# Local products and products with the state trade visits in a gated recurrence beside an MLP

## The chip, the cores and the metric

The kernel runs on 1 core of one Trainium2 chip. The metric is the device time of one execution in microseconds (us). The kernel before takes 926.75 us, the median of 3 runs (925.89 to 927.98).

## The reference

A gated recurrence over 768 steps, for 4 batches and 8 heads of 48, whose output (as 3072 tokens of 384) goes through two MLPs with 2048 hidden columns, the first with softplus, the second with mish. Cut to what matters:

```python
f = 1.0 / (1.0 + np.exp(-f_logit))
for t in range(S):
    state = f[:, :, t, :, None] * state + np.einsum('bhd,bhe->bhde', k[:, :, t], v[:, :, t])
    y[:, :, t] = np.einsum('bhd,bhde->bhe', q[:, :, t], state)
x = y.transpose(0, 2, 1, 3).reshape(B * S, H * D)
h = x @ w_in                                            # first MLP
x = (np.maximum(h, 0.0) + np.log1p(np.exp(-np.abs(h)))) @ w_out
h = x @ w_in                                            # second MLP, its own weights
sp = np.where(h > 20.0, h, np.log1p(np.exp(np.minimum(h, 20.0))))
y = (h * np.tanh(sp)) @ w_out
```

## The kernel before

**The recurrence.** The 768 steps are cut into 6 chunks of 128 (NC); a chunk of one batch is a group g, so there are 24 groups of 8 heads in 4 head pairs, groups 4k to 4k+3 making the chunk k (the first chunk is 0 in the code; the text counts from 1, so groups 8 to 23 are "chunk 3 on"). A group is halved into two times 64 steps. For it the kernel needs the scores of q against k within each half (`a_near`, L469), the state's part of each half, k against v (L480), a running sum of the decayed state and these parts (`mid`, L491, after the first half; `state`, L506, after the second), the masked scores (L497), the local products of masked scores with v (L524) and the products of q with the decayed state `sp` and with `mid` (L532). Local products and products with the state add up in the same PSUM bank.

The matmuls of a group are small, 64 by 64 or less, and run on a quarter of PE's array each, four at a time (`TILES`). Local products take the row half h of the array for the bank h, products with the state the other row half for some. So `a_far` puts a drain of PE (L541) between the two kinds.

**The preparation of a group** is its gate: exponentials of f (ScalarE, `a_exp`), a scan on VectorE (L303) with a reciprocal (L309, `a_scan`), the inverse (ScalarE, `a_inv`), q and k scaled (VectorE, `a_q` L333, `a_k` L339), the state's decay to `sp` (`a_decay`, L354), and the turn: four transposes of k on PE (L403) and a copy by ScalarE to `kn` (L409).

**The MLPs.** The output of four groups is one tile of 512 columns. Each layer goes through 6 such tiles, 16 blocks f of hidden columns each: 96 units a layer, 192 in all. A unit is `m_h` (9 matmuls of 128x512, L636, or plain float32 ones for the first 12 units), its activation on ScalarE and VectorE (L665 to L686 in layer 1), a split into high and low parts (L651, L656), and `m_o` (9 matmuls, L766) of the unit three before, into three accumulators. After 16 units the accumulators are moved out by ScalarE (L786) and VectorE (L787). The tile's input is split into xh (ScalarE) and xl (VectorE, L610, one piece each of three) before `m_h` of the tile's first unit. Chunk k's groups run beside the units of tile k-1, since tile k needs them.

**What sets the order.** A table of hooks: `at(i, place, fn, ...)` puts a step at a place of unit i. Places in a unit come in the order `pe1` (after `m_h`), `act0`, then `m_o`, then `pe2`, then the steps of the activation, then `dve1`, `act`, `dve2`, `pe3`, `end`. From unit 14 (HAND1) the order written is the order on PE, VectorE and ScalarE; before that a scheduler moves instructions. A group of chunk 3 on is planned by `plan_hand(g, i)`, with i from `BASES`: 16, 20, 23, 26 for the first four, then 30, 34, 38, 42 and so on every 16 units. The first visit on PE (`a_near`) stands at `pe2` of unit i, its steps on VectorE (`a_nears`: mid, two masks, state) at `dve2` of unit i, the second visit (`a_far`) at `pe2` of unit i+1. The preparation of g+1 stands at units i to i+3 beside it. `plan_attn` does the same for groups 4 to 7.

Beside these run the loads and the conversion of layer 2's weights to a high and a low part (VectorE, L172, L178, L184). A second path, for gates out of range, is chosen at the end and isn't run here.

Of the kernel before, what the change touches and what calls it, by code (L numbers as in the profile page):

```python
# [8 lines left out]
F32 = mybir.dt.float32  # L9
# [16 lines left out]
R = 112  # L26
HC = C // 2
# [39 lines left out]
def recurrence__then__softplus_mish_mlps_kernel(  # L67
# [10 lines left out]
    nc = tc.nc  # L78
# [8 lines left out]
    const = pool("const")  # L87
# [3 lines left out]
    at_p = pool("at", 2)  # L91
# [6 lines left out]
    ps_o = pool("ps_o", 3, PSUM)  # L98
    ps_a = pool("ps_a", 1, PSUM)

    ident = const.tile([128, 128], F32, name="ident")
    mask = const.tile([128, C], F32, name="mask")
    near = const.tile([128, HC], F32, name="near")
    cap = const.tile([128, NP, C + 1], F32, name="cap")
# [152 lines left out]
    G = {}  # L257
# [84 lines left out]
    def a_decay(g):  # L342
        t = G[g]
        if g < B:
            return
        sp = at_p.tile([R, NP, D], F32, tag="sp", name="sp")
        if g < 2 * B:
            for p in range(NP):
                act.activation(
                    out=sp[:, p], in_=states[g % B][:, p], func=AF.Copy, scale=t["p"][:, p:p + 1]  # L350
                )
            t["sp"] = sp
# [5 lines left out]
        t["sp"] = sp  # L358
# [79 lines left out]
    def a_out(g, pl=None):  # L438
        t = G[g]
        t["yps"] = ps = bank(pl or ps_a, [128, NP, C])  # L440
        for p in range(KD, NP):
            for i in range(2):
# [3 lines left out]
                    start=(p == KD), stop=True,  # L446
                )

    def two_banks(g):
        by_hand = g >= 2 * B  # L450
        return [bank(ps_a, [128, 4 * C], f"a{z}" if by_hand else None) for z in range(2)]
# [8 lines left out]
    TILES = ((0, 0), (1, 1), (0, 1), (1, 0))  # L460

    def a_near(g):

        t = G[g]
        t["xps"] = banks = two_banks(g)
        for p in range(NP):
            for i, h in TILES:
                o, e = 64 * i, 64 * h
                pe.matmul(  # L469
                    banks[i][e:e + HC, p * HC:(p + 1) * HC],  # L470
                    t["k"][o:o + D, p, h * HC:(h + 1) * HC], t["q"][o:o + D, p, h * HC:(h + 1) * HC],
                    start=True, stop=True,
                )
        last = g >= (NC - 1) * B
        for p in range(NP):
            for h, i in TILES:
                if last and h:
                    continue
                o, e, m = 64 * i, 64 * h, D if i else 64
                pe.matmul(  # L480
                    banks[h][o:o + m, NP * HC + p * D:NP * HC + (p + 1) * D],
                    t["kn"][e:e + HC, p, o:o + m],
                    t["v"][e:e + HC, (2 * p + i) * D:(2 * p + i + 1) * D],
                    start=True, stop=True,
                )

    def a_first(g):
        t = G[g]
        t["mid"] = mid = at1.tile([R, NP, D], F32, tag="kn", name="mid")
        part = t["xps"][0][:R, NP * HC:NP * (HC + D)].rearrange("r (p d) -> r p d", p=NP)  # L490
        dve.tensor_tensor(out=mid, in0=t["sp"], in1=part, op=ALU.add)  # L491

    def a_near_mask(g, i):
        t = G[g]
        if i == 0:
            t["a"] = at_p.tile([128, 2, NP, HC], F32, tag="a", name="a")
        dve.tensor_tensor(  # L497
            out=t["a"][:, i], in0=t["xps"][i][:, 0:NP * HC].rearrange("s (p t) -> s p t", p=NP),
            in1=near.rearrange("s (o t) -> s o t", o=1).to_broadcast([128, NP, HC]), op=ALU.mult,
        )  # L500

    def a_second(g):
        t = G[g]
        if g < (NC - 1) * B:
            part = t["xps"][1][:R, NP * HC:NP * (HC + D)].rearrange("r (p d) -> r p d", p=NP)
            dve.tensor_tensor(out=states[g % B], in0=t["mid"], in1=part, op=ALU.add)  # L506
# [7 lines left out]
    def a_far(g):  # L514

        t = G[g]
        t["yps"] = banks = two_banks(g)

        def to(h, o, p, n):
            return banks[h][64 * o:64 * o + n, p * HC:(p + 1) * HC]  # L520

        def local(h, o, p):
            i, e = h ^ o, 64 * h
            return pe.matmul(  # L524
                to(h, o, p, 64), t["v"][e:e + HC, (2 * p + i) * D:(2 * p + i) * D + 64],
                t["a"][e:e + HC, i, p], start=(p == 0), stop=False,
            )

        def far(h, o, p):
            i = h ^ o  # L530
            e = 64 * i
            return pe.matmul(  # L532
                to(h, o, p, D), t["mid" if h else "sp"][e:e + D, p],
                t["q"][e:e + D, p, h * HC:(h + 1) * HC], start=False, stop=(p == NP - 1),
            )

        for p in range(NP):
            for o in (1, 0):
                for h in range(2):
                    done = local(h, o, p)  # L540
        gap = pe.drain()  # L541
        order_only(gap, done)
        for p in range(NP):
            for o in (1, 0):
                for h in range(2):
                    order_only(far(h, o, p), gap)

    def a_rest(g):
        t = G[g]
# [39 lines left out]
                nc.sync.dma_start(out=x[64 * i + 48:64 * i + 64, kk], in_=x[o:o + 16, KD])  # L589

    states = [const.tile([R, NP, D], F32, name=f"state{b}") for b in range(B)]


    xh, xl = {}, {}
# [228 lines left out]

    def plan_attn(g, i):

        at(i, "pe1", a_turn, g)
        at(i, "pe1", a_turned, g)
        at(i, "pe2", a_near, g)
        at(i, "pe2", a_nears, g)
        at(i + 1, "pe2", a_far, g)  # L830
        at(i + 2, "act0", a_outed, g)
        if g + 2 < NC * B:
            at(i + 2, "dve2", a_load, g + 2)

    def plan_hand(g, i):

        close = g < 3 * B
        at(i - 1, "pe3" if close else "pe1", a_turn, g)
        if g == 2 * B:
            at(i - 1, "end", a_turned, g)  # L840
        else:
            at(i if close else i - 1, "act0" if close else "act", a_turned, g)
        at(i, "pe2", a_near, g)
        at(i, "dve2", a_nears, g)
        at(i + 1, "pe2", a_far, g)
# [4 lines left out]
        if g == NC * B:  # L850
            at(i + 3, "dve1", judge)
            return
# [7 lines left out]
        at(i + 3, "dve1", a_decay, g)  # L860

    def plan_split(k):
        if k == 1:
# [4 lines left out]
        for kk in range(KD):  # L868
            at(k * NF - 3 + (kk > 0), "act", split_xa, (1, k), kk)
            at(k * NF - 2 + (kk > 0), "dve2" if kk == 0 else "dve1", split_xb, (1, k), kk)  # L870

    for k in range(2, n1):
        for j in range(B):
            plan_hand(k * B + j, k * NF + BASES[k > 2][j])
        i = k * NF
        at(i - 4, "act", a_fill, k)
        plan_split(k)
# [81 lines left out]
    for o in (0, 64):  # L959
        nc.gpsimd.tensor_copy(out=near[o:o + HC], in_=mask[o:o + HC, o:o + HC])  # L960
    sel = st_p.tile([128, KD, 128], F32, tag="raw", name="sel")
    nc.gpsimd.memset(sel, 0.0)

# [34 lines left out]
    with tc.manual_schedule(engines=HAND | {mybir.EngineType.SP}):  # L998
        for step in HEAD.split():
            one(step)  # L1000
    run(-1, "act0")
    run(-1, "act")

# [289 lines left out]
```

## Time and profile before

| | |
|---|---|
| median of 3 runs | 926.75 us (925.89 to 927.98) |
| the profiled execution | 925.63 us |
| its span | 923.9 us |
| PE busy | 903.1 us (98%) |
| VectorE (DVE) busy | 779.2 us (84%) |
| ScalarE (ACT) busy | 757.2 us (82%) |
| GpSimd (POOL) busy | 23.7 us (3%) |
| drains of PE (L541) | 20 |

The profile is of one execution; its span is the time from the first to the last instruction, 1.7 us less than the execution's own time. PE's clock was granted in full all through. An engine's idle time before an instruction is put down to whatever released it last. Matmuls overlap and their ends are modelled, so a standstill of PE is read from the starts of two matmuls.

### The profile page before, as it was taken

What the parts mean: (1) busy time and instruction counts of PE and PEld (TensorE: products, weight loads), DVE (VectorE), ACT (ScalarE), POOL (GpSimd) and SP (SyncE); (2) the same over time, 40 slices, a digit from 0 to 9 for tenths busy, and PEclk for the clock granted to TensorE, in tenths of its full rate; (3) what the DMA queues carried; (4) which work ended last, traced back from release to release, by engine and by line L of the source; (5) the groups of instructions that cost most, each with busy time, mean ns of one, the idle gap of its engine ahead of it and who ended that gap; (6) DMA issues with size and microseconds to landing.
All of it is one profiled execution on the core that took longest, in us unless ns stands there. A gap on an engine that the chain in (4) does not pass through costs nothing.

```text
span 923.9 us, 16281 instructions
## 1 busy us (share of the span) xinstructions
PE 903.1 (98%) x6238; PEld 704.5 (76%) x6238; DVE 779.2 (84%) x1263; ACT 757.2 (82%) x1365; POOL 23.7 (3%) x68
## 2 busy tenths in 40 slices
PE   9899998999999999999999999999999999999997
PEld 8444576777887777788888888888888888888885
DVE  8999998888889889897987898887877878877875
ACT  5887799888888888897878888877878887887875
POOL 0000000000000000000012200000000000000000
PEclk9999999999999999999999999999999999999999
DMA  9999523125345345533497660201101002000001
GB/s 309 348 358 324 181 97 109 49 78 189 132 150 182 108 143 169 181 123 112 169 325 257 226 219 5 98 1 52 52 1 69 35 1 70 34 1 1 35 1 38
DMA packets 32822, 116.19 MB, mean 126 GB/s; under 512 B 4096, under 2 KB 7168, under 8 KB 32736
## 3 DMA queue, kind: packets, MB, share of 16 engines
q1 hardware_dynamic: 27552, 96.19, 30.7%
q0 software_dynamic: 5184, 18.88, 6.3%
q8 instruction: 51, 0.84, 0.4%
q14 instruction: 35, 0.29, 0.1%
HBM read 90.48 MB, written 23.59 MB: 123 GB/s over the span
## 4 chain that ended last, share of the span: by engine, by line
PE 80%; DVE 10%; ACT 6%; issue 2%; DMA 1%; SPq 0%; DVEq 0%; ACTq 0%
PE po L766 38%; PE ps L636 36%; DVE d L673 1%; DVE d L679 1%; PE ps L469 1%; PE busy L981 1%; ACT e L666 1%; PE ps L532 1%; ACT d L667 1%; PE ps L524 1%; ACT e L665 1%; PE ps L403 1%; PE ps L480 1%; DVE w L226 1%; DMA win<-in_w_dram 1%
## 5 line engine op out<-in xcount | busy, mean ns | idle before, releaser
L636 PE MATMUL ps<-x,w 128*128 128x512 f32 x864 | 214.0, 392 | 0.0
L766 PE MATMUL po<-ghi,w 128*128 128x512 f32 x744 | 195.7, 394 | 3.2 <-DVE o L787 3.1
L636 PEld LDWEIGHTS ps<-x,w 128*128 128x128 f32 x864 | 162.3, 188 | 36.9
L636 PE MATMUL ps<-xh,w 128*128 128x512 f32 x504 | 175.2, 402 | 0.0
L766 PEld LDWEIGHTS po<-ghi,w 128*128 128x128 f32 x744 | 138.5, 188 | 34.5 <-DVE o L787 4.9
L766 PE MATMUL po<-g,w 128*128 128x512 f32 x504 | 126.1, 394 | 0.0
L700 ACT ACTIVATE l<-d 128x512 f32<-128x512 f32 x96 | 60.7, 632 | 68.6 <-DVE d L696 68.6
L636 PEld LDWEIGHTS ps<-xh,w 128*128 128x128 f32 x504 | 94.6, 188 | 22.3 <-issue 0.7
L766 PEld LDWEIGHTS po<-g,w 128*128 128x128 f32 x504 | 94.9, 188 | 21.5
L766 PE MATMUL po<-glo,w 128*128 128x512 f32 x372 | 109.0, 392 | 0.0
L636 PE MATMUL ps<-xl,w 128*128 128x512 f32 x252 | 99.0, 393 | 0.4 <-DVE xl L610 0.4
L696 DVE TENSOR_SCALAR d<-ps 128x512 f32<-128x512 f32 x96 | 66.2, 690 | 32.1 <-PE ps L636 32.1
L710 DVE SCALAR_TENSOR_TENSOR l<-d,l 128x512 f32<-128x512 f32 x96 | 66.5, 693 | 31.3 <-ACT l L703 31.0
L665 ACT ACTIVATE e<-ps 128x512 f32<-128x512 f32 x96 | 56.8, 592 | 43.2 <-DVE d L673 25.5
L656 DVE TENSOR_TENSOR glo<-l,ghi 128x512 fp32r<-128x512 f32 x124 | 85.1, 686 | 6.2 <-ACT ghi L651 5.9
L766 PEld LDWEIGHTS po<-glo,w 128*128 128x128 f32 x372 | 69.9, 188 | 15.4
L651 ACT CAST ghi<-l 128x512 fp32r<-128x512 f32 x124 | 75.0, 605 | 4.4 <-DVE l L686 4.0
L673 DVE SCALAR_TENSOR_TENSOR d<-d,e 128x512 f32<-128x512 f32 x96 | 65.7, 685 | 9.5 <-ACT d L667 8.6
L733 DVE TENSOR_TENSOR l<-ps,l 128x512 f32<-128x512 f32 x96 | 66.3, 691 | 8.5 <-ACT l L730 0.4
L679 DVE TENSOR_TENSOR d<-l,d 128x512 f32<-128x512 f32 x96 | 65.8, 686 | 0.1
L725 DVE SCALAR_TENSOR_TENSOR l<-d,l 128x512 f32<-128x512 f32 x96 | 65.4, 682 | 0.0
L666 ACT ACTIVATE e<-e 128x512 f32<-128x512 f32 x96 | 60.7, 632 | 2.8
(124 smaller groups left out, 1305.1 us busy)
## 6 DMA issues: line engine op xcount, KB each, us to landing
raw<-in_w_dram SPq DMA_DIRECT2D x32, 768.0 KB, 7.3
win<-in_w_dram SPq DMA_DIRECT2D x17, 767.9 KB, 7.2
raw<-in_w_dram SPq DMA_DIRECT2D x15, 767.9 KB, 12.0
qk<-in_qkT_dram SPq DMA_DIRECT2D x22, 448.0 KB, 4.9
x2d<-o SPq DMA_DIRECT2D x12, 768.0 KB, 3.5
w2d<-wo SPq DMA_DIRECT2D x24, 384.0 KB, 2.6
x<-x2d POOLq DMA_DIRECT2D x12, 768.0 KB, 5.5
w<-w2d POOLq DMA_DIRECT2D x24, 384.0 KB, 4.1
```

What stands on the lines that cost most here:

```text
L636: pe.matmul(ps, w, r, start=(i == 0), stop=(i == len(steps) - 1))
L651: act.copy(out=t["hi"], in_=t["g"])
L656: dve.tensor_tensor(out=t["lo"], in0=t["g"], in1=t["hi"].bitcast(F32), op=ALU.subtract)
L665: act.activation(out=e, in_=t["h"], func=AF.Abs)
L666: act.activation(out=e, in_=e, func=AF.Exp, scale=-1.0)
L673: dve.scalar_tensor_tensor(out=d, in0=d, scalar=1.0, in1=t["e"], op0=ALU.subtract, op1=ALU.subtract)
L679: dve.tensor_tensor(out=d, in0=l, in1=d, op=ALU.subtract)
L696: dve.tensor_scalar(out=t["t"], in0=t["h"], scalar1=20.0, scalar2=None, op0=ALU.min)
L710: dve.scalar_tensor_tensor(out=t["l"], in0=t["t"], scalar=-43.0, in1=t["l"], op0=ALU.max, op1=ALU.add)
L725: dve.scalar_tensor_tensor(out=t["l"], in0=t["t"], scalar=-1.0, in1=t["l"], op0=ALU.mult, op1=ALU.max)
L733: dve.tensor_tensor(out=t["l"], in0=t["h"], in1=t["l"], op=ALU.mult)
L766: pe.matmul(acc[c], w[layer, f][:, cols[c]], t[part], start=(f == 0 and part == "hi" and w is whi), stop=(f == NF - 1 and part == "lo"),)
```

## The change

For groups 8 to 23 the two visits of PE are dealt out anew.

- The visit at unit i (`a_one`) has the scores and the products with the state. Both are ready there, since `sp` and `mid` are made earlier.
- The visit at unit i+1 (`a_two`) has the local products and the state parts of the next group, g+1. VectorE's sums (`a_part_sums`: mid and state) follow it, at `dve2` of unit i+1, and are group g+1's.
- So products with the state open the sums in a bank in one visit, and local products close them in the next; there is no drain. The 20 drains become 4, those of groups 4 to 7 (`a_close`).
- The parts of group 8 stand alone in a visit at unit 16 (`a_begin`), and the first i is 17 instead of 16. The last group's second visit has no next parts.
- The products with the state have 64 columns of their stationary instead of 48, so `sp` and `mid` have 16 columns behind them; they become parts of fixed tiles (`sps`, `middle`) that they share with the constants `cap`, `mask` and `ident`, whose names the trace and the order rows then show.
- Everything that prepares a group runs one group further ahead (`plan_ahead(g + 2, i)`), its turn too; that of group 9 stands at unit 13 and is moved by the scheduler.
- q and k of g+2 are loaded at the end of unit i, v at the end of unit i+1 (both at `dve2` of unit i+2 before).
- Groups 5 to 7 have their turn and their first visit half a unit to a unit earlier.

```diff
-BASES = ((-16, -12, -9, -6), (-18, -14, -10, -6))
+BASES = ((-15, -12, -9, -6), (-18, -14, -10, -6))
...
-    def a_nears(g):
-        a_first(g)
-        a_near_mask(g, 0)
-        a_near_mask(g, 1)
-        a_second(g)
...
+    def a_begin(g):
+
+        a_parts(g, two_banks(g))
+
+    def a_one(g):
+
+        G[g]["yps"] = banks = two_banks(g)
+        a_near(g, banks, W)
+        for p in range(NP):
+            for h, o in ORDER:
+                far(g, h, o, p, True)
+
+    def a_two(g):
+
+        for p in range(NP):
+            for h, o in ORDER:
+                local(g, h, o, p)
+        if g + 1 < NC * B:
+            a_parts(g + 1, G[g]["yps"])
...
-    def plan_hand(g, i):
-
-        close = g < 3 * B
-        at(i - 1, "pe3" if close else "pe1", a_turn, g)
...
-        at(i, "pe2", a_near, g)
-        at(i, "dve2", a_nears, g)
-        at(i + 1, "pe2", a_far, g)
-        at(i + 2, "act0", a_outed, g)
-        if g + 2 < NC * B:
-            at(i + 2, "dve2", a_load, g + 2)
-        g += 1
...
+    def plan_ahead(g, i):
+
         at(i - (i % NF == 2), "act", a_exp, g)
         at(i + 1, "dve1", a_scan, g)
         at(i + 1, "act", a_inv, g)
...
+    def plan_hand(g, i, after):
+
+        if g == 2 * B:
+            at(i - 2, "pe1", a_turn, g)
+            at(i - 2, "act", a_turned, g)
+            at(i - 1, "pe2", a_begin, g)
+            at(i - 1, "dve2", a_part_sums, g)
...
+        at(i, "pe2", a_one, g)
+        at(i, "dve2", a_near_masks, g)
...
+        at(i + 1, "pe2", a_two, g)
+        if g + 1 < NC * B:
+            at(i + 1, "dve2", a_part_sums, g + 1)
...
+        if g + 2 < NC * B:
+            plan_ahead(g + 2, i)
+            close = after == i + 3
+            at(after - 1, "pe3" if close else "pe1", a_turn, g + 2)
```

PE before, the second visit of a group of chunk 4 (`a` are masked scores, `vt` is v; the drain between the two kinds isn't listed):

```order
L766 MATMUL po<-ghi,w 128x512 x6
L766 MATMUL po<-glo,w 128x512 x3
L524 MATMUL ps<-a,vt 64x64 x16
L532 MATMUL ps<-qk,sp 48x64
L532 MATMUL ps<-qk,mid 48x64
L532 MATMUL ps<-qk,sp 48x64
```

PE with the change, the end of the first visit of such a group and the second visit (`cap` and `ident` stand for the state and mid behind them):

```order
L531 MATMUL ps<-qk,cap 64x64
L672 MATMUL ps<-xh,w 128x512
L672 MATMUL ps<-xl,w 128x512
L672 MATMUL ps<-xh,w 128x512 x2
L672 MATMUL ps<-xl,w 128x512
L672 MATMUL ps<-xh,w 128x512 x2
L672 MATMUL ps<-xl,w 128x512
L672 MATMUL ps<-xh,w 128x512
L802 MATMUL po<-ghi,w 128x512 x6
L802 MATMUL po<-glo,w 128x512 x3
L521 MATMUL ps<-a,vt 64x64 x16
L477 MATMUL ps<-vt,kn 64x48
```

The products with the state have gone a unit ahead of the local products, with 18 big matmuls between, and the state parts follow the local products.

VectorE before, at the end of a tile (units 46 to 48, a chunk boundary; `gg` is the scan's result). One xl stands just ahead of these rows:

```order
L491 TENSOR_TENSOR mid<-sp,ps 112x192
L497 TENSOR_TENSOR a<-ps,near 128x256 x2
L506 TENSOR_TENSOR state_109<-mid,ps 112x192
L172 TENSOR_TENSOR wo<-raw 128x768
L178 TENSOR_SCALAR raw<-wo 128x768
L184 SCALAR_TENSOR_TENSOR wo<-win,raw 128x768
L673 SCALAR_TENSOR_TENSOR d<-d,e 128x512
L656 TENSOR_TENSOR glo<-l,ghi 128x512
L679 TENSOR_TENSOR d<-l,d 128x512
L686 SCALAR_TENSOR_TENSOR l<-ps,d 128x512
L610 TENSOR_TENSOR xl<-x,xh 128x512 x2
L303 SCALAR_TENSOR_TENSOR gg<-f,cap 112x516
```

VectorE with the change, the same place. The two masks (L509) stand just ahead of these rows, and the state's sum (L490) just behind:

```order
L646 TENSOR_TENSOR xl<-x,xh 128x512
L177 TENSOR_TENSOR wo<-raw 128x768
L183 TENSOR_SCALAR raw<-wo 128x768
L189 SCALAR_TENSOR_TENSOR wo<-win,raw 128x768
L709 SCALAR_TENSOR_TENSOR d<-d,e 128x512
L692 TENSOR_TENSOR glo<-l,ghi 128x512
L715 TENSOR_TENSOR d<-l,d 128x512
L722 SCALAR_TENSOR_TENSOR l<-ps,d 128x512
L308 SCALAR_TENSOR_TENSOR gg<-f,cap 112x516
L314 RECIPROCAL tots<-gg 112x4
L646 TENSOR_TENSOR xl<-x,xh 128x512 x2
L488 TENSOR_TENSOR ident<-mask,ps 112x192
```

The masks stand ahead of the first xl, the scan and its reciprocal ahead of the other two, and the two sums behind them.

VectorE before, ahead of the first tile's accumulators (unit 19):

```order
L333 TENSOR_TENSOR qk<-qk,gg 112x512
L339 TENSOR_TENSOR qk<-qk,f 112x512
L240 TENSOR_TENSOR w<-w_624,w 128x768
L673 SCALAR_TENSOR_TENSOR d<-d,e 128x512
L787 TENSOR_TENSOR o<-po,o 128x512 x3
```

VectorE with the change, the same place:

```order
L308 SCALAR_TENSOR_TENSOR gg<-f,cap 112x516
L314 RECIPROCAL tots<-gg 112x4
L245 TENSOR_TENSOR w<-w_619,w 128x768
L488 TENSOR_TENSOR ident<-mask,ps 112x192
L490 TENSOR_TENSOR state_109<-ident,ps 112x192
L709 SCALAR_TENSOR_TENSOR d<-d,e 128x512
L823 TENSOR_TENSOR o<-po,o 128x512 x3
```

A scan, of group 10, and the sums of group 9 stand ahead of the accumulators' move; the scan of group 9 and its q and k stand further up.

## Rows read from the trace of the kernel before

**Rows 1.** The page: busy engines (share of span), and the chain that ended last

```profile
PE 903.1 (98%) x6238; PEld 704.5 (76%) x6238; DVE 779.2 (84%) x1263; ACT 757.2 (82%) x1365; POOL 23.7 (3%) x68
...
PE 80%; DVE 10%; ACT 6%; issue 2%; DMA 1%; SPq 0%; DVEq 0%; ACTq 0%
```

**Rows 2.** Timeline of PE, both visits of one group (start us, length us, engine, line, tiles)

```profile
242.62 0.69 PE L469 MATMUL ps<-qk 48*64 48x64 f32 x32
243.14 0.63 PE L480 MATMUL ps<-vt,kn 64*64 64x48 f32 x32
243.70 0.51 PE L636 MATMUL ps<-xh,w 128*128 128x512 f32 x1
...
248.04 0.69 PE L524 MATMUL ps<-a,vt 64*64 64x64 f32 x32
248.88 0.25 PE L532 MATMUL ps<-qk,sp 48*48 48x64 f32 x1
...
249.47 0.51 PE L636 MATMUL ps<-xh,w 128*128 128x512 f32 x1
```

**Rows 3.** The drain's line: duration min/median/max in ns, first and last start

```profile
L541 PEldq DRAIN  x20: 516/587/615, 47.9 to 429.5; - x20
```

**Rows 4.** Timelines of PE and VectorE, unit 19 [idle before <- released by]

```profile
142.66 0.74 PE L766 MATMUL po<-ghi,w 128*128 128x512 f32 x2 [2.20 <-DVE o L787]
...
141.92 1.89 DVE L787 TENSOR_TENSOR o<-po,o 128x512 fp32r<-128x512 f32 x3 [0.82 <-ACT o L786]
```

**Rows 5.** Timeline of PE, standstills around three chunk boundaries

```profile
289.73 0.63 PE L636 MATMUL ps<-xh,w 128*128 128x512 f32 x2
290.55 0.50 PE L636 MATMUL ps<-xl,w 128*128 128x512 f32 x1 [0.19 <-DVE xl L610]
...
295.70 0.39 PE L636 MATMUL ps<-xh,w 128*128 128x512 f32 x1
296.42 0.57 PE L403 MATMUL ps<-ident,qk 112*128 112x112 f32 x4 [0.34 <-DMA win<-in_w_dram]
296.77 1.40 PE L766 MATMUL po<-ghi,w 128*128 128x512 f32 x5
...
225.09 0.39 PE L636 MATMUL ps<-xh,w 128*128 128x512 f32 x1
225.91 0.74 PE L766 MATMUL po<-ghi,w 128*128 128x512 f32 x2 [0.43 <-DVE o L787]
...
370.69 0.63 PE L636 MATMUL ps<-xh,w 128*128 128x512 f32 x2
371.23 0.51 PE L636 MATMUL ps<-xl,w 128*128 128x512 f32 x1
...
386.83 0.39 PE L636 MATMUL ps<-xh,w 128*128 128x512 f32 x1
387.35 0.74 PE L766 MATMUL po<-ghi,w 128*128 128x512 f32 x2
```

**Rows 6.** Timeline of VectorE, a scan and what follows its reciprocal

```profile
132.51 1.22 DVE L303 TENSOR_TENSOR_SCAN gg<-f,cap 112x516 f32<-112x516 f32 x1
...
133.87 0.93 DVE L240 TENSOR_TENSOR w<-w,w 128x768 fp32r<-128x768 f32 x1
```

**Rows 7.** Timeline of VectorE, a chunk boundary from the first visit's end

```profile
283.62 0.35 DVE L491 TENSOR_TENSOR mid<-sp,ps 112x192 f32<-112x192 f32 x1 [0.68 <-PE ps L480]
283.89 0.75 DVE L497 TENSOR_TENSOR a<-ps,near 128x256 f32<-128x256 f32 x2
284.56 0.34 DVE L506 TENSOR_TENSOR state<-mid,ps 112x192 f32<-112x192 f32 x1
284.82 0.95 DVE L172 TENSOR_TENSOR wo<-raw 128x768 fp32r<-128x768 f32 x1
...
289.81 1.28 DVE L610 TENSOR_TENSOR xl<-x,xh 128x512 fp32r<-128x512 f32 x2
291.01 1.23 DVE L303 TENSOR_TENSOR_SCAN gg<-f,cap 112x516 f32<-112x516 f32 x1
```

More of the change, by code (lines that the diff above doesn't have):

```diff
@@ L99, in recurrence__then__softplus_mish_mlps_kernel, with behind @@
     ps_a = pool("ps_a", 1, PSUM)
[L101 to L104, printed above, removed]
+    def behind(n, name):
+        both = const.tile([128, NP * D + n], F32, name=name)
+        return both[:R, 0:NP * D + 16], both[:, NP * D:]
+    middle, ident = behind(128, "ident")
+    sp1, mask = behind(C, "mask")
+    sp0, cap = behind(NP * (C + 1), "cap")
+    cap = cap.rearrange("s (p t) -> s p t", p=NP)
+    sps = [sp0, sp1]
     tots = const.tile([128, NC * B, NP], F32, name="tots")
@@ L357, in a_decay @@
         )
-        t["sp"] = sp
     n_a = [0]
@@ L447, in a_out, with chained @@
                 )
+    TILES = ((0, 0), (1, 1), (0, 1), (1, 0))
+    W = NP * HC
+    def chained(g):
+        return g >= 2 * B
     def two_banks(g):
-        by_hand = g >= 2 * B
-        return [bank(ps_a, [128, 4 * C], f"a{z}" if by_hand else None) for z in range(2)]
+        return [bank(ps_a, [128, 4 * C], f"a{z}" if chained(g) else None) for z in range(2)]
     def order_only(x, y):
@@ L458, in order_only, with a_parts @@
         )
-    TILES = ((0, 0), (1, 1), (0, 1), (1, 0))
-    def a_near(g):
+    def a_parts(g, banks):
         t = G[g]
[L465 to L474, printed above, removed]
+        t["sps"] = banks
         for p in range(NP):
             for h, i in TILES:
-                if last and h:
+                if g >= (NC - 1) * B and h:
                     continue
@@ L480, in a_near, with a_part_sums @@
                 pe.matmul(
-                    banks[h][o:o + m, NP * HC + p * D:NP * HC + (p + 1) * D],
-                    t["kn"][e:e + HC, p, o:o + m],
-                    t["v"][e:e + HC, (2 * p + i) * D:(2 * p + i + 1) * D],
+                    banks[h][o:o + m, W + p * D:W + (p + 1) * D], t["kn"][e:e + HC, p, o:o + m],
+                    t["v"][e:e + HC, (2 * p + i) * D:(2 * p + i + 1) * D], start=True, stop=True,
+                )
+    def a_part_sums(g):
+        t = G[g]
+        parts = [
+            x[:R, W:W + NP * D].rearrange("r (p d) -> r p d", p=NP) for x in t["sps"]
+        ]
+        mid = heads_of(middle)
+        dve.tensor_tensor(out=mid, in0=heads_of(t["sp"]), in1=parts[0], op=ALU.add)
+        if g < (NC - 1) * B:
+            dve.tensor_tensor(out=states[g % B], in0=mid, in1=parts[1], op=ALU.add)
@@ L484, in a_near @@
+    def a_near(g, banks, at_col):
+        t = G[g]
+        t["aps"] = [x[:, at_col:at_col + W].rearrange("s (p t) -> s p t", p=NP) for x in banks]
+        for p in range(NP):
+            for i, h in TILES:
+                o, e, half = 64 * i, 64 * h, slice(h * HC, (h + 1) * HC)
+                z = i ^ h if chained(g) else i
+                pe.matmul(
+                    t["aps"][z][e:e + HC, p], t["k"][o:o + D, p, half], t["q"][o:o + D, p, half],
                     start=True, stop=True,
@@ L485, in a_near, with a_near_masks @@
                 )
-    def a_first(g):
+    def a_near_masks(g):
         t = G[g]
[L489 to L493, printed above, removed]
-        t = G[g]
[L495 to L499, printed above, removed]
+        t["a"] = at_p.tile([128, 2, NP, HC], F32, tag="a", name="a")
+        for z in range(2):
+            dve.tensor_tensor(
+                out=t["a"][:, z], in0=t["aps"][z],
+                in1=mask[:, 0:HC].rearrange("s (o t) -> s o t", o=1).to_broadcast([128, NP, HC]),
+                op=ALU.mult,
+            )
@@ L500, in a_near_mask, with to, local, far @@
+    def to(g, h, o, p, n):
+        return G[g]["yps"][h][64 * o:64 * o + n, p * HC:(p + 1) * HC]
+    def local(g, h, o, p, first=False):
+        t = G[g]
+        i, e = h ^ o, 64 * h
+        return pe.matmul(
+            to(g, h, o, p, 64), t["v"][e:e + HC, (2 * p + i) * D:(2 * p + i) * D + 64],
+            t["a"][e:e + HC, o if chained(g) else i, p],
+            start=first and p == 0, stop=not first and p == NP - 1,
         )
-    def a_second(g):
+    def far(g, h, o, p, first=False):
@@ L503, in a_second @@
         t = G[g]
-        if g < (NC - 1) * B:
-            part = t["xps"][1][:R, NP * HC:NP * (HC + D)].rearrange("r (p d) -> r p d", p=NP)
-            dve.tensor_tensor(out=states[g % B], in0=t["mid"], in1=part, op=ALU.add)
-    def a_nears(g):
-        a_first(g)
-        a_near_mask(g, 0)
-        a_near_mask(g, 1)
-        a_second(g)
[L514 to L535, printed above, removed]
+        i = h ^ o
@@ new lines, in far, with a_open, a_opened, a_close @@
+        e = 64 * i
+        return pe.matmul(
+            to(g, h, o, p, 64), (middle if h else G[g]["sp"])[e:e + D, p * D:p * D + 64],
+            t["q"][e:e + D, p, h * HC:(h + 1) * HC],
+            start=first and p == 0, stop=not first and p == NP - 1,
+        )
+    ORDER = ((0, 0), (1, 0), (1, 1), (0, 1))
+    def a_open(g):
+        banks = two_banks(g)
+        a_near(g, banks, 0)
+        a_parts(g, banks)
+    def a_opened(g):
+        a_part_sums(g)
+        a_near_masks(g)
+    def a_close(g):
+        G[g]["yps"] = two_banks(g)
@@ L537, in a_far @@
         for p in range(NP):
-            for o in (1, 0):
-                for h in range(2):
-                    done = local(h, o, p)
+            for h, o in ORDER:
+                done = local(g, h, o, p, True)
         gap = pe.drain()
@@ L543, in a_far @@
         for p in range(NP):
-            for o in (1, 0):
-                for h in range(2):
-                    order_only(far(h, o, p), gap)
+            for h, o in ORDER:
+                order_only(far(g, h, o, p), gap)
+    def a_begin(g):
[4 more added lines that the diff above has]
+        for p in range(NP):
+            for h, o in ORDER:
+                far(g, h, o, p, True)
+    def a_two(g):
+        for p in range(NP):
+            for h, o in ORDER:
+                local(g, h, o, p)
+        if g + 1 < NC * B:
+            a_parts(g + 1, G[g]["yps"])
     def a_rest(g):
@@ L1000, in recurrence__then__softplus_mish_mlps_kernel @@
             one(step)
+    nc.gpsimd.tensor_copy(out=mask[HC:C, 0:HC], in_=mask[HC:C, HC:C])
     run(-1, "act0")
```

41 lines of the change are left out of this document (23 added, 18 removed).

## The prediction

> **What bounds the kernel now.** I read the page's busy times and chain first, then the chain's own engine in order of time, then the instructions that it waits for. TensorE (PE) is busy 98% of the span and carries 80% of the chain that ended last; VectorE (DVE) is busy 84% and carries 10% [rows 1]. So whatever shortens PE's stream should show in the time, unless PE then arrives early at something that DVE delivers. Both parts matter here, and they have to be priced apart.
>
> In the timeline of one group the reader is to see three things [rows 2]. The first visit goes from 242.62 to the next 512-column matmul at 243.70: 0.52 us of scores, 0.56 of state parts, 1.08 together, with no gap where the one kind of tile follows the other. The second goes from 248.04 to 249.47, 1.43 us. Each of the two holds 32 records of small matmuls, then 32 more; the difference is 0.35. In the second, the first product with the state starts 0.84 after the first local product, where the scores need 0.52 before the parts start; that 0.32 is the drain. The drain's own row says 0.59 [rows 3], but a part of it runs while the local products are still going through, so 0.59 is not the price.
>
> PE's standstills are the second thing, read as start to start between 512-column matmuls, which follow each other every 0.23 us. The column of idle time in the rows understates them, since matmul ends are modelled.
>
> **The change, part by part.**
>
> *The drain.* In groups 8 to 23 it goes. A group then has scores (0.52) and products with the state (248.88 to 249.47, 0.59) in the one visit, local products (0.52, taken as the scores, since they have as many records and as many columns) and parts (0.56) in the other: 2.19 against 1.08 + 1.43 = 2.51 [rows 2]. That is **0.32 us a group**. The products with the state now have a stationary of 64 columns instead of 48, which by the scores' pace (0.52 for 32 records of that width) costs nothing. The ends are nothing, if the array has to empty anyway, and 0.59, the drain's row; 0.32 is what the row nearest to the operation gives.
>
> *Where it counts.* The saving of group 8 lies ahead of the standstill at 142.66, where PE waits 2.20 us for VectorE to move the finished accumulators (L787) out [rows 4]. So does the added visit for the parts of group 8 alone, 0.56 us and its entry: the standstill covers both (without that cover the visit would cost its 0.56). Behind it 15 groups are left: 15 x 0.32 = **-4.8**. The last group's second visit has no next parts: **-0.56**. One more turn (transposes, L403) is made ahead of the standstill instead of behind it, 296.42 to 296.77: **-0.35** [rows 5].
>
> *The early standstill.* The preparation now runs one group further ahead. Ahead of L787 VectorE gets a scan with reciprocal more (132.51 to 133.87: 1.36 [rows 6]), the decay of a state (0.26, as the sum of that shape) and the two part sums of group 9 (0.27 + 0.26 [rows 7]): 2.15 us. In front of L787 VectorE stood idle for 0.82, waiting for ScalarE's casts (L786) [rows 4], so up to 1.3 of it should reach PE. The ends are nothing and 2.15, all of it; I take **+1.0**, since VectorE hardly has another gap there, but the order ahead of unit 14 is the scheduler's and may win something back.
>
> *The chunk boundaries (units 30 to 35, 46 to 51, 62 to 67).* This is the counter-effect. Layer 1's inputs for the next chunk are split there, and PE's first unit of the chunk needs xl (L610). Before, VectorE did after the first visit: mid 0.27, two masks 0.67, the state sum 0.26, the weight preparation and a unit's steps 4.99 (284.82 to 289.81), then two xl, the first done after 0.69, and only then the scan [rows 7]: 6.88 from 283.62 until the first of them. Now mid and state sum go behind (-0.53), one xl moves in from ahead of the masks (+0.60, one of the two in 289.81 to 291.01) and the scan with its reciprocal stands ahead of the two xl (+1.36): 8.31, that is 1.43 later, counted from the end of the one visit. VectorE starts this list at that end, as it did before (0.68 idle, released by the visit's last matmul). PE comes 0.32 earlier, since no drain lies between. So the standstill at xl grows by 1.75. It was 0.36 at 290.55 (289.73 plus two steps of 0.23 makes 290.19) and 0.08 at 371.23 [rows 5]. The third boundary has no state sum in the old order, so only 0.27 goes behind there: +2.01. Together 1.75 + 1.75 + 2.01 = 5.5.
>
> Some of it comes back, because PE then arrives late at two later waits that it had to sit through before: the turn (296.42 instead of 295.93, 0.49) and the accumulators (225.91 instead of 225.32, 0.59; at the third boundary 387.35 instead of 387.06, 0.29) [rows 5]. VectorE's work up to there is no longer than before, so these vanish: 3 x 0.49 + 2 x 0.59 + 0.29 = 2.9. What remains is **+2.6**. The ends are 0, if VectorE runs ahead there, and 5.5, if nothing comes back.
>
> *A rule that speaks against the change.* VectorE's old wait ended with the first visit's last parts, not with its scores [rows 7]. In the new first visit the masks would have their scores after 0.52, and the products with the state fill 0.59 more. The Trainium skill's page PSUM — Partial Sum Buffer, section on bank collisions, asks to guard by bank and quadrant and not by address, so the masks have to stand behind the whole visit, as their old neighbours did; by addresses alone they could go 0.59 earlier and the three standstills would be shorter by up to that, some -1.8, and the sum below -3.9 instead of -2.1. The rows and the order of waits go with the rule.
>
> *What costs nothing.* Loads of q and k are issued at the end of the unit and used two units later by VectorE; what covers them is the work of the unit between, over 5 us (242.62 to 248.04 from one visit to the next [rows 2]), and part of the one after it. If that did not hold, VectorE would stand at q. ScalarE gets its copies and inverses in another order, with its total unchanged but for the shift by a group.
>
> **The sum.** -4.8 - 0.56 - 0.35 + 1.0 + 2.6 = -2.1 us. The profiled execution took 925.63 us, so 923.5; the median of the runs shown lies 1.1 above it, at 926.75, so the forecast on that scale is **924.6**.
>
> **The rivals.**
>
> *The saving shows nearly whole.* If VectorE gains on its list (its steps wait for ScalarE in places, and it has 16% idle), the scan is done while it would have stood idle, and the standstills stay as they were: -4.8 - 0.56 - 0.35 + 1.0 = -4.7, or -5.7 without the early term: 921.0 to 922.0. For it speaks that VectorE is idle for 0.68 just before the list [rows 7]; against it that within the list there is no idle time at all.
>
> *VectorE's added and moved work is paid in full; slower.* The place is VectorE's queue at unit 19 and at the three boundaries: the 2.15 and the 5.5 both reach PE, and nothing comes back at turn and accumulators because VectorE stays late there too. 2.15 - 0.35 - 4.8 - 0.56 + 5.5 = +1.9: **928.7**. It decides once less than about 0.1 of the 2.9 comes back. For it: the list after the visit has no slack. Against it: VectorE's work from the visit to the accumulators' move is shorter than before by the sums that went behind.
>
> *The drain's time stays.* If the array empties anyway between two such sets of products, the 4.8 is not there and the rest stands: +2.7, 929.5. Against it: scores and parts pass into each other without a gap [rows 2], and no sum of two row tiles in one bank is left within one visit.
>
> **How the numbers follow.** A difference of over 0.2% (1.85 us) can be told from none. My forecast has a chance of 0.55; with terms that are sure to some 1.5 us, about half of it lies beyond 1.85 faster (under 924.9), nearly all the rest within. The whole saving has 0.25, all of it faster. VectorE's full price has 0.15, half of it over the bound, and the drain that stays 0.05, all slower. Faster 0.25 + 0.28 = 0.53; slower 0.05 + 0.09 = 0.14; same 0.33. The range reaches from 920.9 (the whole saving with no early loss) to 928.7 (the full price); the last rival lies outside. The forecast's own range is 923.1 to 926.1.
>
> **What would show it.** No drain rows but those of chunk 2 (4 of 20). First and second visit of a group 1.1 us each. At the first unit of chunks 3 to 5 a standstill of about 2 us released by VectorE's xl, with the scan's row just ahead of the two xl; no standstill at the turn and the accumulators after it. The accumulators' wait near 142 us about 1 us later. A standstill at xl that stayed at 0.4, or one that came back at the turn, would prove the boundary term wrong; visits of 1.4 us the drain term.

## The result and the profile after

The changed kernel takes **934.75 us** (median of 4 runs, 933.42 to 935.87) against 926.55 for the kernel before (4 runs): ratio 1.0086, 95% interval [1.0068, 1.0104]. That is 8 us slower, where 2 us faster was forecast. The profiled execution took 935.01 us, its span 933.3.

The page after, answering to [rows 1], with the group of xl's matmuls (mean ns of one | idle before, released by):

```profile
PE 907.1 (97%) x6238; PEld 708.1 (76%) x6238; DVE 779.2 (83%) x1263; ACT 757.6 (81%) x1365; POOL 24.0 (3%) x67
...
PE 79%; DVE 11%; ACT 6%; issue 2%; DMA 1%; SPq 0%; ACTq 0%; DVEq 0%
...
L672 PE MATMUL ps<-xl,w 128*128 128x512 f32 x252 | 99.9, 396 | 5.7 <-DVE xl L646 5.7
```

PE has the same 6238 matmuls and no drains from group 8 on, yet is busy 4 us longer. The list of PE's waits after (total us, times, longest) starts with these three and one of 2.8, for weights, that the kernel before has too. Before, the three came to 0.4, nothing and 0.6 in total:

```profile
PE ps L672 <- DVE xl L646: 5.7, 3, 1.9
...
PE ps L406 <- DVE state L490: 2.6, 1, 2.6
PE ps L406 <- DVE qk L344: 2.2, 1, 2.2
```

The first is the one forecast, at three chunk boundaries. PE's timeline of the changed kernel at the first of them, answering to [rows 5]:

```profile
214.61 0.63 PE L672 MATMUL ps<-xh,w 128*128 128x512 f32 x2
217.15 0.50 PE L672 MATMUL ps<-xl,w 128*128 128x512 f32 x1 [1.91 <-DVE xl L646]
...
218.18 0.39 PE L672 MATMUL ps<-xh,w 128*128 128x512 f32 x1
218.41 2.70 PE L802 MATMUL po<-ghi,w 128*128 128x512 f32 x6
220.90 1.31 PE L802 MATMUL po<-glo,w 128*128 128x512 f32 x3
222.05 0.40 PE L672 MATMUL ps<-xh,w 128*128 128x512 f32 x1
```

PE should have gone on at 215.07 and does at 217.15: a standstill of 2.08. Then something that was not forecast: the nine `po` matmuls last from 218.41 to 222.05, 3.6 us, where nine steps of 0.23 are 2.1. VectorE's timeline at the same place, answering to [rows 7], shows the cause of the standstill:

```profile
208.78 0.75 DVE L509 TENSOR_TENSOR a<-ps,mask 128x256 f32<-128x256 f32 x2 [2.65 <-PE ps L531]
209.46 0.68 DVE L646 TENSOR_TENSOR xl<-x,xh 128x512 fp32r<-128x512 f32 x1
...
212.51 0.68 DVE L709 SCALAR_TENSOR_TENSOR d<-d,e 128x512 f32<-128x512 f32 x1
...
215.04 1.22 DVE L308 TENSOR_TENSOR_SCAN gg<-f,cap 112x516 f32<-112x516 f32 x1
...
216.40 1.29 DVE L646 TENSOR_TENSOR xl<-x,xh 128x512 fp32r<-128x512 f32 x2
```

The first of the two xl is done some 8.3 us after the visit's end at 208.78, as the sum in the prediction has it; the scan stands just ahead. The matmuls' length after it is read from the granted clock. Stretches of the changed kernel (bounds in us, length, busy us of PE, PEld, DVE, ACT, POOL, PE's granted clock, DMA share, GB/s), around unit 16 and the second boundary:

```profile
128.00:131.60 3.60, 0.96 (x34) 0.56 (x33) 3.46 (x8) 3.54 (x7) 0.00 (x0) 1.00 0.24 64
131.60:137.00 5.40, 5.40 (x19) 4.37 (x20) 4.17 (x6) 3.39 (x6) 0.00 (x0) 0.68 0.00 0
137.00:145.00 8.00, 8.00 (x154) 6.30 (x153) 5.72 (x11) 6.66 (x13) 0.11 (x1) 1.00 0.21 61
...
297.00:300.00 3.00, 1.09 (x5) 0.60 (x4) 2.97 (x6) 2.84 (x5) 0.00 (x0) 1.00 0.93 286
300.00:304.00 4.00, 4.00 (x12) 3.08 (x12) 3.86 (x9) 3.49 (x8) 0.00 (x0) 0.57 0.55 228
```

PE stands, starts again at the full 2.4 GHz, and a little later runs for some 3 us at 1.2 GHz. Seven 512-column matmuls a time start 0.43 apart instead of 0.23, and an eighth in part, so some 1.6 us are lost behind each of four standstills. This isn't the profiled execution alone: the four executions of the changed kernel have a mean granted clock of 0.990 to 0.994. Of 18 executions of the kernel before on one chip, those at 0.998 and 0.999 took 925.6 to 927.3 us, those at 0.996 and 0.997 took 927.5 to 928.7, and one at 0.994 took 931.3; so the scatter between executions goes with the clock too, and the profiled execution of before had no fall while PE worked.

The other new waits are in the first hand-ordered units. PE's timeline of the changed kernel there, units 16 and 19:

```profile
128.28 0.68 PE L477 MATMUL ps<-vt,kn 64*64 64x48 f32 x32
131.60 0.60 PE L406 MATMUL ps<-ident,qk 112*128 112x112 f32 x4 [2.64 <-DVE state L490]
...
146.75 0.73 PE L802 MATMUL po<-ghi,w 128*128 128x512 f32 x2
...
148.71 0.40 PE L802 MATMUL po<-glo,w 128*128 128x512 f32 x1
151.27 0.57 PE L406 MATMUL ps<-ident,qk 112*128 112x112 f32 x4 [2.17 <-DVE qk L344]
```

At unit 16 the turn of group 9 follows the visit for group 8's parts and writes a bank that VectorE's state sum (L490) has yet to read. At unit 19 the turn of group 10 asks for VectorE's k in the unit in which it is made. The accumulators' wait of [rows 4] is all but gone (146.75 comes 0.2 after its turn), since PE is late itself.

The shift of the same 512-column matmul between the two traces adds this up: +2.5 at the end of unit 13, +6.4 behind the turn of unit 19 (151.62), +6.0 ahead of the first boundary; then +2.2, +2.2 and +2.8 across the three boundaries (from the first matmul of units 32, 48 and 64 to the move of the accumulators), and -1.0, -1.0 and -1.9 between and behind them, where the visits' saving shows: +9.3 at the end.

### The profile page after: what moved, and what is told of

It is laid out like the page before. It is cut to its first block, busy times and chain, and to the rows that moved or that the text cites. A ratio compares the mean times of both kernels' runs of the same rounds, so it can differ in the third digit from the quotient of the medians.

```text
span 933.3 us, 16223 instructions
## 1 busy us (share of the span) xinstructions
PE 907.1 (97%) x6238; PEld 708.1 (76%) x6238; DVE 779.2 (83%) x1263; ACT 757.6 (81%) x1365; POOL 24.0 (3%) x67
## 4 chain that ended last, share of the span: by engine, by line
PE 79%; DVE 11%; ACT 6%; issue 2%; DMA 1%; SPq 0%; ACTq 0%; DVEq 0%
PE po L802 37%; PE ps L672 36%; DVE gg L308 1%; PE ps L500 1%; DVE d L709 1%; DVE d L715 1%; ACT e L702 1%; ACT e L701 1%; PE ps L406 1%; PE ps L531 1%; DVE xl L646 1%; ACT d L703 1%; DVE w L231 1%; DVE raw L220 1%; DVE l L722 1%
## 5 line engine op out<-in xcount | busy, mean ns | idle before, releaser
L802 PE MATMUL po<-ghi,w 128*128 128x512 f32 x744 | 199.7, 400 | 0.0
L802 PEld LDWEIGHTS po<-ghi,w 128*128 128x128 f32 x744 | 141.6, 192 | 31.8 <-DVE o L823 1.2
```

Of the source, the lines that this page charges most:

```text
L802: pe.matmul(acc[c], w[layer, f][:, cols[c]], t[part], start=(f == 0 and part == "hi" and w is whi), stop=(f == NF - 1 and part == "lo"),)
```

## The experiments

Ratios are to the kernel before, timed on the same chip. The first 120 us of a profiled execution differ between executions: up to the end of unit 13 the traces of the changed kernel and of runs 1, 2, 3 and 9 have the same program, and their shift to the trace of before there is 2.5, 6.0, 1.4, 1.0 and 0.9 us. So traces are compared by stretches behind it, and times by medians.

**1. The scan back behind xl.** Groups and splits are planned chunk by chunk. On VectorE this moves the three xl of a boundary and nothing else; on ScalarE two casts to xh move ahead of the gate's two steps beside them.

```diff
-    for j, i in enumerate(spots[:-1]):
-        plan_hand(2 * B + j, i, spots[j + 1])
     plan_ahead(2 * B + 1, 13)
     for k in range(2, n1):
+        for j in range(B):
+            n = (k - 2) * B + j
+            plan_hand(k * B + j, spots[n], spots[n + 1])
```

> The changed kernel with the splits (xl) planned chunk by chunk beside the groups, as before, so that VectorE's order at a chunk boundary is again xl, masks, weights, steps, two xl, and only then the scan; the two part sums stay behind. Theory A (the scan ahead of xl keeps PE waiting 2.1 us at the first unit of chunks 3 to 5, and the standstill then drops PE's clock for some 3 us, which costs 1.5 more): both go, some 1.1 a boundary comes back at the turn and the accumulators, so 3 x (2.0 + 1.5 - 1.1) = 7 us less, about 927.5, granted clock 1.00 from 195 us on. Rival B (VectorE sets the time there whatever the order; the wait only moves to the turn and the accumulators): less than 2 us gained, 933 or more. Rival C (the clock falls for another reason, such as the new visits): the standstills go, 3 x 0.9 = 3 us gained, and the clock's dips of 0.66 to 0.72 stay after the second visit.

Measured: 929.64 us (11 runs), ratio 1.0021 [1.0009, 1.0032], so 6.0 us off the loss of 8, where 7 were expected. The profiled execution took 934.7, the longest of the eleven: its clock fell at 44.8, 137.0 and 157.5 us. PE's timeline at the first boundary:

```profile
221.03 0.63 PE L672 MATMUL ps<-xh,w 128*128 128x512 f32 x2
221.59 0.51 PE L672 MATMUL ps<-xl,w 128*128 128x512 f32 x1
...
226.77 0.39 PE L672 MATMUL ps<-xh,w 128*128 128x512 f32 x1
228.19 0.57 PE L406 MATMUL ps<-ident,qk 112*128 112x112 f32 x4 [1.03 <-ACT l L704]
```

The standstill at xl falls to 0.1, the turn's grows to 1.2, the clock stays at 1.00 from 195 us on. From the second visit of unit 31 to the first of unit 34 it is 15.42 us before, 17.86 with the change, 15.52 here; 2.3 gained at each of the first two boundaries and 2.8 at the third. Theory A holds; B and C fall. That the standstill and the clock go together here doesn't yet show which drives which; run 2 does.

**2. Useless matmuls in the standstill.** VectorE's order is the changed kernel's.

```diff
+        if layer == 1 and f == 0 and k in (2, 3, 4):
+            for _ in range(8):
+                pe.matmul(ps, steps[0][0], steps[0][1], start=True, stop=True)
```

> The changed kernel with eight more 512-column matmuls ahead of the first unit's own in chunks 3 to 5; they write the accumulator that the unit's first matmul then overwrites, so they add 8 x 0.23 = 1.8 us of work that does nothing, in front of a wait of 2.1 us. VectorE's order is untouched. Theory A (the clock falls because PE stands still): the same xl arrives at the same time, the clock stays at 1.00, and 3 to 4.5 us are gained with more work: 930 to 931.5. Rival C (the clock falls for another reason): no gain, 934 to 936, dips as before. Rival D (added work costs its time): 3 x 1.8 = 5.5 more, 940.

Measured: 932.90 us (4 runs), ratio 1.0074 [1.0045, 1.0104], an interval too wide to tell it from the changed kernel by itself, and outside the 930 to 931.5 that A gave: in the profiled execution the wait at unit 16 was longer (3.3 us from start to start instead of 2.9) and the clock was down for 6.8 us there, so that it lost 2.5 us more up to unit 18. The stretches tell: 16.26, 16.25 and 16.26 us from unit 31 to 34 and at the two places like it, against 17.86, 17.84 and 17.83. PE's timeline and the granted clock at the first of them:

```profile
215.50 2.12 PE L673 MATMUL ps<-xh,w 128*128 128x512 f32 x8
...
217.92 0.62 PE L675 MATMUL ps<-xh,w 128*128 128x512 f32 x2
218.63 0.50 PE L675 MATMUL ps<-xl,w 128*128 128x512 f32 x1
...
218.00:222.00 4.00, 3.92 (x18) 2.90 (x17) 3.86 (x8) 3.38 (x8) 0.00 (x0) 1.00 0.74 282
```

24 more matmuls, and each boundary is 1.6 us shorter. xl comes when it came; what is gained is the clock, which fell at none of the three. With the same standstill and no filling, in the changed kernel and runs 3 and 4, it fell at eight of nine. So theory A holds for the mechanism though its time was missed, C and D fall: the clock fell because PE stood.

**3. Three turns behind nine matmuls.**

```diff
-            at(after - 1, "pe3" if close else "pe1", a_turn, g + 2)
+            at(after if close else after - 1, "pe1", a_turn, g + 2)
```

> The changed kernel with the turns of groups 10 to 12 moved from the end of a unit (pe3 of unit 19, 22, 25) to behind the next unit's first nine matmuls (pe1 of unit 20, 23, 26). Theory A (PE stands 2.2 us at 149 and about 0.5 at 167 and 183 because the first spot is a unit later and the turn in the same unit asks for VectorE's k, which comes last there): about 3 us gained, 931.5. Rival B (VectorE is late anyway, and the next thing that it delivers is waited for): under 1 us gained; the wait turns up at the next visit, for ScalarE's copy of the turn.

Measured: 931.66 us (9 runs), ratio 1.0051 [1.0033, 1.0069], so 3.2 us gained by ratio; the wait of 2.2 us is gone and none takes its place. A holds. Its trace gave more than was asked, since the order at the boundaries is the changed kernel's. Stretches at the first and second boundary:

```profile
211.00:214.00 3.00, 1.08 (x4) 0.58 (x3) 2.97 (x6) 2.78 (x5) 0.00 (x0) 0.89 1.01 362
214.00:217.00 3.00, 3.00 (x9) 2.35 (x8) 2.86 (x6) 2.10 (x5) 0.00 (x0) 0.54 0.55 224
...
292.00:295.00 3.00, 1.74 (x49) 1.17 (x40) 2.93 (x6) 2.88 (x6) 0.11 (x1) 1.00 1.03 324
295.00:300.00 5.00, 4.32 (x19) 3.52 (x20) 4.86 (x11) 4.38 (x9) 0.00 (x0) 1.00 0.60 237
```

The same order and the same standstill, with a fall of the clock at the first and none at the second: 17.77 against 16.35 us. So the clock's part of this boundary is 1.4 us, and it isn't lost every time; at the third boundary it fell again (17.85).

**4. The lone visit a unit earlier.**

```diff
-            at(i - 2, "pe1", a_turn, g)
-            at(i - 2, "act", a_turned, g)
-            at(i - 1, "pe2", a_begin, g)
-            at(i - 1, "dve2", a_part_sums, g)
+            at(i - 3, "pe3", a_turn, g)
+            at(i - 2, "act0", a_turned, g)
+            at(i - 2, "pe2", a_begin, g)
+            at(i - 2, "dve2", a_part_sums, g)
```

> The changed kernel with the visit for the parts of group 8 alone, its sums and its turn a unit earlier (unit 15 instead of 16). Theory A (PE stands 2.6 us at 129 to 131.6 because the turn of group 9 follows in the same unit and writes the bank that VectorE's sum still has to read, and the clock falls behind it): the standstill and the dip near 133 go, 2.5 to 4 us gained, 931 to 932. Rival B (VectorE sets the time up to the accumulators at 146 anyway): under 1 us gained, the wait comes back there.

Measured: 934.36 us (4 runs), ratio 1.0067 [1.0042, 1.0093]: 1.8 us better by ratio, and the intervals overlap. PE's timeline:

```profile
124.68 0.68 PE L477 MATMUL ps<-vt,kn 64*64 64x48 f32 x32 [2.12 <-ACT kn L412]
...
129.53 0.55 PE L406 MATMUL ps<-ident,qk 112*128 112x112 f32 x4
```

The wait for the sum went and one for ScalarE's copy of group 8's turn came in the unit before. The edit was badly placed; neither theory had that.

**5 to 7. Edits 1, 3 and 4 together, then with a drain, then with groups 5 to 7 as before.**

```diff
         a_near(g, banks, W)
+        gap = pe.drain()
         for p in range(NP):
             for h, o in ORDER:
-                far(g, h, o, p, True)
+                order_only(far(g, h, o, p, True), gap)
```

> The changed kernel with three of the edits together: splits planned beside the groups (scan behind xl), the turns of groups 10 to 12 behind the next unit's first nine matmuls, and the visit for group 8's parts a unit earlier. Theory A (standstills made by the order, and the clock that falls behind them, are the whole loss; the visits themselves save 0.35 us a group): the sum of the three, about 3 to 5 us under the kernel before (ratio 0.995 to 0.997), granted clock 1.00 from 130 us on. Rival B (VectorE's added work up to the accumulators near 142 us comes through whatever the order): about the kernel before, ratio 0.999 to 1.001.

Measured: 922.32 us (6 runs), ratio 0.9946 [0.9933, 0.9959]: 5 us faster than the kernel before. Theory A holds; the granted clock is 1.00 from 130 us on. The wait of 2.1 us for the copy of group 8's turn, known from run 4, is still there (at 124.86), here with a fall of the clock from 125.0 to 128.4. One group of chunk 4 in PE's timeline, answering to [rows 2]:

```profile
242.53 0.69 PE L500 MATMUL ps<-qk 48*64 48x64 f32 x32
243.05 0.23 PE L531 MATMUL ps<-qk,cap 48*64 48x64 f32 x2
...
243.62 0.50 PE L672 MATMUL ps<-xh,w 128*128 128x512 f32 x1
...
247.95 0.69 PE L521 MATMUL ps<-a,vt 64*64 64x64 f32 x32
248.47 0.62 PE L477 MATMUL ps<-vt,kn 64*64 64x48 f32 x32
249.02 0.51 PE L672 MATMUL ps<-xh,w 128*128 128x512 f32 x1
```

> The kernel with those three edits, and a drain put back in each first visit of groups 8 to 23, between the scores and the products with the state; nothing else differs, so this measures the drain by itself. Theory A (a drain costs what the two visits differed by, 0.32 us): each first visit 0.32 longer, 16 x 0.32 = 5 us more than without, less what standstills after it give back. Rival B (the drain's own row, 0.59): 9 us more. Rival C (the array empties there anyway): within 1 us.

Measured: 927.64 us (12 runs), ratio 1.0005 [0.9992, 1.0017]. The drain alone costs 5.3 us between the medians, 0.33 each: theory A, and with it the whole lead over the kernel before is gone. In PE's timeline the products with the state start 0.81 after the scores, where they started 0.52 after them:

```profile
244.40 0.69 PE L500 MATMUL ps<-qk 48*64 48x64 f32 x32
245.21 0.26 PE L531 MATMUL ps<-qk,cap 48*64 48x64 f32 x1
```

> The kernel with those three edits, and groups 5 to 7 planned as before the change (turn at pe1, first visit at pe2 of the same unit). Theory A (their earlier places do not matter, because the stretch up to 100 us is set by loads and VectorE): within 1 us of the kernel with three edits. Rival B (they delay the first tile's units): 1 to 2.5 us less.

Measured: 922.80 us (5 runs), ratio 0.9952 [0.9939, 0.9965]: no difference, A.

**8. The kernel before, with only the scan ahead of xl.**

```diff
         for j in range(B):
             plan_hand(k * B + j, k * NF + BASES[k > 2][j])
+    for k in range(2, n1):
         i = k * NF
         at(i - 4, "act", a_fill, k)
         plan_split(k)
```

> The kernel BEFORE with only the order at the chunk boundaries of the changed one: the splits planned after all groups, so that the scan with its reciprocal stands ahead of the two xl on VectorE; visits and drains untouched. Theory A (the order alone makes the standstill): PE waits 0.4 + 1.4 = 1.7 us at xl in chunks 3 to 5 instead of 0.4, 1.36 more, of which 1.1 comes back at turn and accumulators; and where the clock falls behind it, 1.5 more: 0.3 to 1.8 a boundary, 1 to 5 us in all. Rival B (without the change's other moves VectorE catches up): within 1 us of the kernel before.

Measured: 935.46 us (6 runs), ratio 1.0083 [1.0067, 1.0098]. Eight us, more than the 1 to 5 expected, with no change of the visits: at each boundary the edit moves the scan, its reciprocal and one xl on VectorE, and on ScalarE the gate's two steps ahead of two casts to xh and a copy by one place; VectorE runs through to the last xl without idle time, so its own order sets the wait. Each standstill grew by 1.97, not 1.36, since here one xl moved behind the masks too; 0.5 came back at the turn; and at the second boundary the clock cost 1.6. That makes 6.0 at the boundaries of the profiled execution. Another 1.6 was lost to the clock at unit 19, which the edit doesn't touch. PE's timeline at the second boundary and at unit 19, and the stretch behind unit 19's wait:

```profile
297.11 0.50 PE L636 MATMUL ps<-xl,w 128*128 128x512 f32 x1 [2.19 <-DVE xl L610]
...
144.28 0.88 PE L766 MATMUL po<-ghi,w 128*128 128x512 f32 x2 [2.21 <-DVE o L787]
...
145.00:148.00 3.00, 3.00 (x9) 2.23 (x8) 2.96 (x6) 2.39 (x5) 0.00 (x0) 0.50 0.92 375
```

The wait at unit 19 is that of [rows 4], 2.20 there and 2.21 here, behind the same instructions: the clock held in the one trace and fell in the other. At the boundaries of this trace it fell at one of three.

**9. The lone visit left at unit 16, the turn behind it moved.** With edits 1 and 3:

```diff
-            at(i - 1, "pe3", a_turn, g + 1)
+            at(i, "pe1", a_turn, g + 1)
```

> The kernel with the splits beside the groups and the turns of groups 10 to 12 behind nine matmuls, and the visit for group 8's parts left at unit 16; instead the turn of group 9, which follows it in the same unit, goes to pe1 of unit 17, behind nine matmuls too. Theory A (PE stands there for VectorE's sums of those parts, which the nine matmuls of 2.1 us cover): the standstill of 2.6 us at unit 16 falls below 0.8, no slow clock from 120 us on, and the time is that of the kernel with three edits or up to 2 us less: ratio 0.992 to 0.995. Rival B (what stands ahead of the accumulators at 145 us is VectorE's work, wherever PE waits): the accumulators' wait grows by what is gained, within 0.5 us of the kernel with three edits. Rival C: the first visit of group 8 then waits for the copy of that turn on ScalarE, 1 to 2 us, and the time is 1 us more than the kernel with three edits.

Measured: **921.65 us** (6 runs), ratio 0.9938 [0.9919, 0.9958], the fastest of all and ahead of both kernels. The wait at unit 16 in PE's timeline, and the stretch of chunks 3 to 6:

```profile
131.29 0.60 PE L406 MATMUL ps<-ident,qk 112*128 112x112 f32 x4 [0.77 <-DVE state L490]
...
195.00:437.00 242.00, 238.93 (x2364) 190.44 (x2363) 209.17 (x358) 205.94 (x369) 1.47 (x11) 1.00 0.42 146
```

The wait falls from 2.64 to 0.77, and the clock never falls while PE works; A holds. The accumulators' wait is 0.33 and none for the turn's copy appears at group 8's first visit, so B and C fall. Against the three edits of run 5 the gain isn't clear (the intervals overlap).

## Why the prediction was wrong

**The drain, right.** 0.32 a group was taken; the two visits take 1.09 + 1.07 = 2.16 instead of 2.51, and putting the drain back costs 0.33. It saves about 5 us, and shows in full once nothing stands in its way (runs 5 and 9).

**The boundaries' standstills, right in place, cause and size; the term's price was wrong.** The xl came 8.3 us after the visit, PE stood 2.08 instead of 0.36, and the shift to the kernel before grew there by 1.70, 1.74 and 2.01 (forecast 1.75, 1.75 and 2.01); 0.5 came back at each turn, 0.6, 0.6 and 0.3 at the accumulators, 2.9 in all as forecast. That the masks stand behind the whole visit was right too: they read the scores alone and were released by the last products with the state (L531, at 208.78). [rows 7] couldn't show this, since mid, which stands first there, reads the parts that end the old visit. Where the clock held (run 3, second boundary) the stretch from unit 31 to 34 was 0.93 longer than before. What failed is "What remains is +2.6": the step behind it assumed that PE, once it goes on, goes on at full rate. It didn't, and 1.6 us a boundary came on top, 4.7 in all. The trace of before showed a standstill of 2.2 us with the clock at 1.00 behind it, and the prediction has no term and no rival for the clock. Run 8 has the same standstill with the clock at 0.50. The Trainium skill says on its page TensorE: Matmul & The Clock Gate, in the section on HAM oscillation, that waits between pieces of work can put PE back to half rate so that the next piece starts cold. The traces agree that a wait can be followed by half rate, with 1.4 to 1.6 us lost behind waits of 1.9 us or more; they differ in that the next piece mostly started at full rate and slowed within it, up to 1.5 us later. That a standstill costs more than its length was a rival that should have stood in the prediction.

**The early stretch, wrong.** "I take +1.0", and "the standstill covers both" for the lone visit, with 0.35 off for the turn: +0.65. It measured +6.4 by 151.6 us: +2.5 at the end of unit 13; the wait of 2.6 us at unit 16 with 1.6 of slow clock; the wait of 2.2 at unit 19; less about 2 that came back at the accumulators. The +2.5 is for the most part this execution's own: the clock fell at 92.2 in it, behind a wait of 1.6 us that the same program has in run 3 without a fall (0.57 against 1.00 below), and runs 2, 3 and 9 show 0.9 to 1.4 there. Run 8's trace, whose program up to there is that of the kernel before, shows 1.6 against the trace of before, so the change's own part can't be told from scatter. The windows of the changed kernel, then of run 3:

```profile
92.00:96.00 4.00, 4.00 (x6) 1.67 (x7) 4.00 (x10) 3.57 (x6) 0.00 (x0) 0.57 1.00 274
...
92.00:96.00 4.00, 4.00 (x10) 1.71 (x9) 4.00 (x10) 3.57 (x6) 0.00 (x0) 1.00 1.01 332
```

The failed step counted VectorE's added work and not what PE asks of it: I priced the turns as PE work that moves, and did not follow the first spot's move from 16 to 17 to the place where turn and k meet in one unit, nor ask who reads the bank that the next turn writes. Turns of groups 11 and 12 waited 0.45 longer at the same spot; there the trace names ScalarE's activation (L703), not VectorE's k. VectorE's added work, for which +1.0 was taken, hardly reached PE once these waits were gone: in run 9 the accumulators' wait is 0.33 instead of 2.20, and the shift to the kernel before is +0.1 at the start of unit 20.

**The rivals.** The whole saving (921.0 to 922.0) isn't what the change as made gave, but about what it gives once its standstills are gone (922.32 in run 5, 921.65 in run 9). That the drain's time stays is refuted by run 6. The slower one named the right queue, VectorE's at unit 19 and the boundaries, and the wrong price: 928.7, without the clock. Its claim that nothing comes back is wrong; the turn and the accumulators gave back what was forecast.

**Still open** is what decides whether the clock falls behind a given standstill: of waits of 1.9 to 2.6 us it fell behind four of five with the change, two of three at run 3's boundaries, and differed between two executions at the same instruction. Between 100 and 870 us the eleven traces have 26 places where 2.2 us or more pass between the starts of two matmuls. The clock fell at 19 of them and nowhere else in that stretch; it held at all 13 places where 1.15 to 1.6 us pass. Part of the first 120 us' scatter is also not explained.

## What to carry to other kernels

Where one table of hooks sets several engines' order, moving a loop that fills it reorders steps at equal places; here the scan ahead of two xl, with one xl behind the masks, cost 8 us by itself (run 8). When a change takes PE work out, list for each later PE instruction what it waits for and which reader must leave its bank. In this kernel a PE standstill of about 2 us cost its length and, in 19 of 26 cases, about 1.5 us more; if it can't be removed, give PE work to do in it.

## What the runs showed of the hardware

Behind a standstill the granted clock fell to 0.50, mostly for about 3 us. In the changed kernel it fell 0.7 to 1.5 us after PE had gone on, as at 218.5 behind the standstill that ended at 217.15; in run 2 it was already down at 130.9, ahead of PE's start at 131.8. Eight useless 512-column matmuls in a wait (1.8 us) made the stretch 1.6 us shorter. A drain's own row of 0.59 [rows 3] has cost 0.33.
